# Score banks counted as free before a change of tiling in a build-time search, and the V weights on another queue

## The chip, the cores and the metric

The kernel runs on one core of one Trainium2 chip. The metric is the device time of one execution in microseconds; less is better. The core's engines are TensorE (matrix products; PE in the profile, with its weight loads as PEld), ScalarE (ACT), VectorE (DVE), GpSimd (POOL) and SyncE (SP, which here only issues DMAs). Each engine works through its own queue in order, and the engines wait for one another through semaphores.

## The reference

```python
x = A_x                                        # 1 x 2048 x 512, bf16
g = sigmoid((x * gate_w).sum(-1, keepdims=True))
q, k, v = (x @ wqkv) split into 32 heads of 16
a = softmax(q @ k.T / sqrt(16)) @ v, heads joined, @ wo
b = ((x @ w_gate) * (x @ w_up)) @ w_down       # inner width 1376
return g * a + (1 - g) * b
```

It is attention with 32 small heads over 2048 tokens beside a gated MLP, mixed by a gate per token. The matrix of probabilities has 32 x 2048 x 2048 entries, and every one of them needs an exponential: that is the bulk of the work of ScalarE and VectorE.

## The kernel before

**Units.** The scores are worked out in units of 128 keys by 512 queries for one head. One unit fills one PSUM bank (`ps` has eight; seven, `NPOOL`, are shared by everything, and the eighth, `OB`, collects the output of PV). A group `m` (32 of them, `NG`) is four heads `j` by 512 queries, with 16 blocks of keys `kt`, so there are 2048 units.

**Bursts.** Since a head has only 16 channels, TensorE runs up to four units side by side in row tiles of 32x128 (the matmul at L907, in `burst`). The mode is called "row". Everything else, the projections and the MLP (`run_fill`, matmul at L427) and PV (`pv_pack`, L1100), runs in four column tiles of 128x32, the mode "col". A spare lane of a burst can take a quarter of a product with `wo` (L433).

**Exponentials.** A unit's scores leave PSUM in one of two ways. ScalarE does `Exp` on one bank or on two neighbouring banks in one instruction (`act_step`, L968). VectorE writes a cheap approximation by integer arithmetic (`dve_exp`, L1002), which GpSimd completes with two more shifted copies (`pool_step`, L1051); PV then sums three terms in place of one. 20 or 24 units in 64 go to VectorE (`more`). As soon as the exponential has read the bank, another burst or fill may have it: `give` puts it back into `pool_free`.

**Fills.** The projections of Q, K and V, the MLP and the output products are tiles of 4 to 15 steps (`tiles`, a queue with due dates). Such a tile also holds a bank from its first step until VectorE or ScalarE has read it; at most `FILL_LIM` of them at once.

**The order.** None of this is decided on the chip. While the program is built, `_Clock` plays the engines against each other with fixed durations: a step of TensorE takes `MM` = 216 ns and `SWITCH` = 108 ns more when it changes its tiling, a result is seen `SEM` = 55 ns after its end, an exponential of n banks takes 51 + 427n ns on ScalarE and 600 ns on VectorE. Whenever an engine is free, its step function (`pe_step`, `act_step`, `dve_step`, `pool_step`) lists what it may do next, in an order of preference that constants set, and `choose` takes the entry that the next digit of `ORDER` names (0 is the first). `ORDER` was found by a search at the writer's desk. What comes out is a fixed list of instructions for each engine, with the semaphores that the data need:

```python
def ready(self, o):
    return o is not None and o.t1 + self.SEM <= self.now + 1e-6
```

An engine of the chip doesn't follow the planned times, only the planned order, and it waits on semaphores where the data are late. A burst carries a wait for each bank, on the instruction that read it last.

**The head.** The input x comes in four blocks (`x0t`, on SP's and ScalarE's queues), is transposed on TensorE with the identity `idn` and copied to `xT`; then the first Q (`wq0`) and K weights (`wk0`), then V's (`wv`), then the later x by transposing DMAs (L354 issues all loads):

```python
load("sp", "wq0", wq[:, :, 0:128], wcol(0, 128), lat=4200)
load("act", "wk0", wk[:, :, 0:128], wcol(D, D + 128), lat=4200)
load("act", "wv", wv, wcol(2 * D, 3 * D), lat=5000, prio=7)
```

`lat` is what the plan supposes for the landing. `wa` in the profile is the buffer that holds the K and V weights first and the MLP's inner values later: rows `ps<-xT,wa` are K's projection (or, with the same names, the gate's), `ps<-wa,xT` are V's.

Of the kernel before, what the change touches and what calls it, by code (L numbers as in the profile page):

```python
# [127 lines left out]
class _Clock:  # L128
# [17 lines left out]
    def ready(self, o):  # L146
        return o is not None and o.t1 + self.SEM <= self.now + 1e-6
# [56 lines left out]
def bass_gated_mix__mha_block__glu_gated_bilinear__prompt_kernel(  # L204
# [15 lines left out]
    "1100110010000010110000000000000000000000000000000100000000000000000000400000020000000010002001000000"  # L220
    "0020001000000200000001010003000000010010010000000010000001000000001001000000040000000010030000000200"
    "0000010000000000002000000000010000100000400000000001000000000000000100000000200100000000000000005000"
    "0000030200010000000001000000000001000000000001005000000020000000004000100110002000000000300000010003"
    "0000300003000000003000000100002000002000000200000040000010000000000000000100030000000000020100000001"
    "0000020000120024000000200000000400000000100000000000000000001000000000000001101000000000100000000000"
    "1000000000000000000001000001000000000400000000002000020000001000000000001000000001000100000000000100"
    "5000000000010010110000100000000000100000000000000100000000000001000000000000000000000001000000000101"
    "1100000000000020000000001000000000000000100000000000200000000000000000000100000000000000500000000000"
    "0000000002000020000010100000000000000000100000001010000000000000000000000010100000001000000400100100"
    "0400022000000000000000000000000001000000000010000000100000020000000000001100000000001000000000010000"  # L230
    "0000100100000000020010001000000002000000000002200000000000000000000010201000000000000000000000010000"
    "0000000000000000111000000030001000010040010002000010000200000000000010000000000200000000000001000000"
    "3000000100000000000001100310100000001001000000001000001001000010000001005000000000000000000000101100"
    "1220000053030000000000040000001000002000000100500000000010100000001000001000000000000001000010000000"
    "0000010000000000010000010010000000000000000000000000000000000000000000100000000100000000000001000000"
    "0100000000004000000000000400002000000001000002010000000001010001010000001001001011100000002000000420"
    "0000011010000000000001000000000000000000000000000000000000000000000000000000010000100400010001000100"
    "0000010000000102040000001000002030000000000000320012000100000011000110000500000000000110000000000100"
    "0000200000000000000000000001000000011000010000000000000000010041000000000000100000000000001100001000"
    "0000040000000000001000000000000000001000000230010000100000000001001000010000000000000000000000000111"  # L240
    "0001020000000010000000000000040000001000000000031000300000000000100000001000010000000000000000000000"
    "0100000000000001110000000000000100000000000000000010000000000100000000100100000000002200000400000002"
    "0001000000000100010100010100000200000000021000000000200000000000000000002000010000010000002004000000"
    "0000050010200000000000000020000100100003000000011110010010000003000000000000100010000000000000000000"
    "0000000000000000010000020000200000010001000000000000000000000000010000000000010000000000010000000100"
    "0000010100000000000000000000000000000001000010000001000000000000000000001005000000000000200000001040"
    "0000000000000001002000001000000000000000000040000000000001010000000000000010000000000000000000010000"
    "1000000000000000000001000000000000000010000000001000100000000400000000000000000100000300000500000000"
    "0010001000000000100020000000000002001000000000000010000002001010010000000000000000001000000000101010"
    "1303000053000200000000020000000003000100000101000110100100000001001001000110000000000000000000000"  # L250
# [12 lines left out]
MM, SWITCH, SECOND, MML = 216.0, 108.0, 10.0, 390.0  # L263
# [26 lines left out]
def _build(nc, A_x, A_wqkv, A_wo, W_gate, W_up, W_down, gate_w, out):  # L290
# [8 lines left out]
    with ExitStack() as stack:  # L299
# [59 lines left out]
        load("sp", "wq0", wq[:, :, 0:128], wcol(0, 128), lat=4200)  # L359
        load("act", "wk0", wk[:, :, 0:128], wcol(D, D + 128), lat=4200)  # L360
        load("act", "wv", wv, wcol(2 * D, 3 * D), lat=5000, prio=7)
        t_x = {}
        for ch in range(1, NCH):
            if ch == NCH - 1:
                load("sp", "wk1", wk[:, :, 128:D], wcol(D + 128, 2 * D), lat=6000)
                load("sp", "wq1", wq[:, :, 128:D], wcol(128, D), lat=6500)
                load("sp", "gw", gw[:, :], gate_w.rearrange("(kt p) -> p kt", p=128), lat=6000, allow_slow_non_contiguous=True)
            for kt in range(KD):
                load("sp", f"x{ch}{kt}", xT[:, kt, ch * 512 : (ch + 1) * 512],
                     x2[ch * 512 : (ch + 1) * 512, kt * 128 : (kt + 1) * 128], lat=3900, transpose=True)  # L370
                K.tasks["sp"][-1][4] = 1650.0
# [43 lines left out]
        const("pool", "qz0", lambda g: g.memset(QE[:, :, 1:NB, :].rearrange("p e b n -> p e (b n)").bitcast(F32), 0.0), ["wdz"], 1650, 1700)  # L415
# [23 lines left out]
        pool_free = list(range(NPOOL))  # L439
        fill_n = [0]  # L440
# [382 lines left out]
        def plan_burst(bias):  # L823
# [4 lines left out]
            banks = [b_ for b_ in pool_free]  # L828
# [106 lines left out]


# [6 lines left out]
        def act_step():  # L943
            if K.pick("act", 1):
                return True
            n = min(len(act_ready), len(pt_free) - 2 * y_out[0])
            if n < 0:
                n = 0
            if not n:
                return K.pick("act")  # L950
            us = [act_ready[0]]
            if n > 1:
                near = [x for x in act_ready if abs(x[1] - us[0][1]) == 1]
                if near and choose("a", ["2", "1"]) == "2":
# [9 lines left out]
            def done(o):  # L964
                for (u, bank, _), q in zip(us, cells):
                    give(bank, [o])

            o = K.issue("act", lambda a: a.activation(PT[:, cs, :], ps[:, bs, :], ACT.Exp, scale=math.log(2.0) / 1024.0),  # L968
                        deps, 51.0 + 427.0 * n, 176.0 + 427.0 * n, done)
# [25 lines left out]
        def dve_exp():  # L995
            if not can_dve():
# [6 lines left out]
                        [dep] + pt_rel[y], 600.0, 690.0, lambda o: (give(bank, [o]), pool_add.append((u, y, o))))  # L1003
# [66 lines left out]
        def pv_ready(it):  # L1070
            if not K.ready(it.dep):
                return False
# [4 lines left out]
        def pv_pick():  # L1077
            m = pvm[0]
            if m >= NG or m not in n_dve or not pv_open[0] or not all(K.ready(o) for o in pv_rel[0]):
                return []  # L1080
            r = []
            for j in range(4):
                for it in pvq.get((m, j), ()):
                    if pv_ready(it):
# [144 lines left out]
        def fill_tile():  # L1229

            for i, tl in enumerate(list(tiles)[: FILL_LOOK + 2 * (stat["units"] >= 4 * T * NG)]):
                d = tl.deps()
                ok = d is not None and all(K.ready(o) for o in d)
                if tl.bank is None:
# [5 lines left out]
                    if fill_n[0] < lim and len(pool_free) >= FILL_MIN:  # L1240
                        return tl
# [7 lines left out]
        def fill_begin(tl):  # L1249
            got = sorted(pool_free)  # L1250
# [154 lines left out]
        ACT_CAP, DVE_CAP, BIAS, THR_A, THR_D, LATE, EARLY, FILL_LOOK = 6, 2, 400.0, 800.0, 0.0, 12, 40, 3  # L1405
        FILL_MIN, KMIN, PT_MIN, PV_MIN, FILL_LIM, FF, FF_PT = 1, 3, 9, 4, 2, 1, 8
# [183 lines left out]
```

## Time and profile before

| | us |
|---|---|
| median of three runs | 655.16 |
| lowest, highest | 654.68, 655.42 |
| the profiled execution | 657.29 |
| its span in the profile | 655.7 |
| ScalarE's exponentials, from the first start to the last | 12.7 to 639.3 |

The span is what the profile covers, from the first instruction to the last; the execution's own time has about 1.6 us more. All times inside the profile are in microseconds from the start of the span. A row of the timeline gives the start, the time that it took (of several merged instructions, from the first start to the last end), engine, line, operation, output and inputs, and in brackets the idle time of the engine before it and who ended that. Matmuls overlap, so their own durations (0.38 us) are longer than their distance.

### The profile page before, as it was taken

The page shows a single profiled execution, that of the slowest core. Times are in us where ns is not written, and L with a number is a line of the kernel's source. Part 1 is how long each engine was busy: PE and PEld are TensorE (multiplying, and loading weights), DVE is VectorE, ACT ScalarE, POOL GpSimd, SP SyncE. Part 2 cuts the span into 40 slices and gives each one's busy share as a digit, 9 for nine tenths or more (in the row PEclk, how much of TensorE's full clock was granted, in tenths as well). Part 3 has the DMA queues.
Part 4 walks back from the last instruction along what each step waited for, and adds up shares of the span by engine and source line. Part 5 has one row for each costly group of instructions (what it writes and reads, how often), then busy time and mean ns, then how long its engine had stood idle before and what let it go on. Part 6 is the DMA issues. An engine that isn't in the chain of part 4 may idle for free.

```text
span 655.7 us, 21110 instructions
## 1 busy us (share of the span) xinstructions
PE 647.3 (99%) x8690; PEld 187.3 (29%) x8690; DVE 593.0 (90%) x1000; ACT 629.3 (96%) x772; POOL 542.7 (83%) x1397
## 2 busy tenths in 40 slices
PE   7999999999999999999999999999999999999997
PEld 3332222222222222222222232222222322222233
DVE  5999999999998898989998989999998899999994
ACT  3899999999999999999999999999999999999992
POOL 2479998888988898988788989989897898899890
PEclk8999999999999999999999999999999999999999
DMA  8930201000010100101000010100101010000101
GB/s 153 282 91 6 71 9 35 13 11 27 2 35 2 42 20 17 29 3 35 2 19 30 13 41 10 29 10 7 31 6 40 19 36 2 7 24 2 28 18 36
DMA packets 28659, 21.16 MB, mean 32 GB/s; under 512 B 16488, under 2 KB 24396, under 8 KB 28560
## 3 DMA queue, kind: packets, MB, share of 16 engines
q1 hardware_dynamic: 27216, 18.87, 10.8%
q8 instruction: 68, 1.11, 0.7%
q10 hardware_dynamic: 1344, 0.92, 0.5%
q14 instruction: 31, 0.25, 0.1%
HBM read 11.63 MB, written 2.37 MB: 21 GB/s over the span
## 4 chain that ended last, share of the span: by engine, by line
PE 60%; ACT 37%; DVE 1%; DMA 1%; issue 0%; SPq 0%; DVEq 0%
ACT PT L968 37%; PE ps L1100 21%; PE ps L427 20%; PE ps L907 17%; PE ps L433 3%; DVE PT L1002 1%; DMA wq<-in_A_wqkv_dram 1%; DMA gsm<-gscr 0%; PE ps L1211 0%; DVE gsm L592 0%; SPq L354 0%; DVE oc L1197 0%; ACT QE L710 0%; DVE usb L583 0%; DVE rec L1188 0%
## 5 line engine op out<-in xcount | busy, mean ns | idle before, releaser
L968 ACT ACTIVATE PT<-ps 128x1024 bf16<-128x1024 f32 (+1 forms) x761 | 622.9, 1050 | 5.0 <-PE ps L907 4.6
L1051 POOL INT64_ADD PT<-PT x1386 | 539.8, 409 | 96.0 <-DVE PT L1002 82.6
L1002 DVE TENSOR_SCALAR PT<-ps 128x512 int16<-128x512 f32 x708 | 461.5, 684 | 39.3 <-PE ps L907 26.7
L907 PE MATMUL ps<-QE,KK 32*128 32x512 bf16 x2048 | 253.5, 384 | 0.1
L1100 PE MATMUL ps<-PT,V 128*32 128x512 bf16 (+1 forms) x2048 | 227.9, 384 | 0.0
L1100 PE MATMUL ps<-PT,VS 128*32 128x512 f16 x1416 | 181.2, 384 | 0.0
L907 PEld LDWEIGHTS ps<-QE,KK 32*128 32x128 bf16 x2048 | 65.2, 91 | 236.9 <-ACT PT L968 184.2
L1100 PEld LDWEIGHTS ps<-PT,V 128*32 128x32 bf16 x2048 | 55.0, 95 | 63.0 <-issue 51.4
L1100 PEld LDWEIGHTS ps<-PT,VS 128*32 128x32 bf16 x1416 | 43.6, 95 | 40.6 <-issue 28.6
L427 PE MATMUL ps<-wd,wa 128*32 128x512 bf16 x704 | 54.5, 382 | 0.0
L427 PE MATMUL ps<-xT,wu 128*32 128x512 bf16 x704 | 53.4, 383 | 0.1
L427 PE MATMUL ps<-xT,wg 128*32 128x512 bf16 x704 | 53.3, 383 | 0.0
L622 DVE TENSOR_TENSOR usb<-ps,omg 128x512 bf16<-128x512 f32 x44 | 30.0, 683 | 2.0 <-PE ps L427 1.9
L649 DVE TENSOR_TENSOR wa<-ps,usb 128x512 bf16<-128x512 f32 x44 | 30.1, 683 | 1.4 <-PE ps L427 1.2
L433 PE MATMUL ps<-wo,OT 32*128 32x512 bf16 x80 | 30.8, 384 | 0.2
L427 PE MATMUL ps<-xT,wq 128*32 128x512 bf16 x256 | 20.3, 396 | 2.1 <-DMA wq<-in_A_wqkv_dram 2.1
L427 PE MATMUL ps<-xT,wa 128*32 128x512 bf16 x272 | 21.4, 398 | 0.1
L1197 DVE COPY oc<-ps 128x512 f32<-128x512 f32 x31 | 21.1, 682 | 0.3
L427 PEld LDWEIGHTS ps<-wd,wa 128*32 128x32 bf16 x704 | 15.5, 95 | 19.4 <-issue 11.8
L427 PEld LDWEIGHTS ps<-xT,wg 128*32 128x32 bf16 x704 | 13.8, 95 | 18.7 <-issue 11.3
L427 PEld LDWEIGHTS ps<-xT,wu 128*32 128x32 bf16 x704 | 13.1, 95 | 18.6 <-issue 12.7
L427 PE MATMUL ps<-wa,xT 128*32 128x512 bf16 x256 | 17.8, 384 | 0.0
(73 smaller groups left out, 142.8 us busy)
## 6 DMA issues: line engine op xcount, KB each, us to landing
rb<-rscr SPq DMA_DIRECT2D x16, 256.0 KB
QE<-Qr SPq DMA_DIRECT2D x120, 16.0 KB, 1.8
oc<-oc SPq DMA_DIRECT2D x60, 32.0 KB, 1.9
out_dram<-ost SPq DMA_DIRECT2D x12, 128.0 KB, 1.7
wu<-in_B_w_up_dram SPq DMA_DIRECT2D x1, 1376.0 KB, 7.5
wg<-in_B_w_gate_dram SPq DMA_DIRECT2D x1, 1376.0 KB, 9.6
wd<-in_B_w_down_dram SPq DMA_DIRECT2D x1, 1280.0 KB, 14.0
wa<-in_A_wqkv_dram ACTq DMA_DIRECT2D x1, 512.0 KB, 7.0
```

The costliest lines, as they stand in the source:

```text
L427: r = pe.matmul(ps[32 * i : 32 * i + 32, bank, :], w, x_, start=s0, stop=s1, tile_position=(0, 32 * i), skip_group_check=True)
L433: return pe.matmul(ps[:, bank, :], lhs[32 * q : 32 * q + 32, :], rhs[32 * q : 32 * q + 32, :], start=s0, stop=s1, tile_position=(32 * q, 0 ...
L622: return v.tensor_tensor(usb[:, st["s"], :], ps[:, bank, :], omg[:, cf, :], ALU.mult)
L649: return v.tensor_tensor(hT[:, f, :], ps[:, bank, :], usb[:, u_at[cf, f][0], :], ALU.mult)
L907: return lambda pe: pe.matmul(ps[:, bank, :], KK[32 * j : 32 * j + 32, b, kt * 128 : (kt + 1) * 128], QE[32 * j : 32 * j + 32, p, b, :], s ...
L968: o = K.issue("act", lambda a: a.activation(PT[:, cs, :], ps[:, bs, :], ACT.Exp, scale=math.log(2.0) / 1024.0), deps, 51.0 + 427.0 * n, 17 ...
L1002: o = K.issue("dve", lambda v: v.tensor_scalar(PT[:, y, :].bitcast(I16), ps[:, bank, :], BIAS16, 0.0, ALU.add, ALU.max), [dep] + pt_rel[y] ...
L1051: return g.int64_add(PT[:, zl, :].bitcast(I64), PT[:, sl, :].bitcast(I64), w)
L1100: return lambda pe: pe.matmul(ps[32 * it.j : 32 * it.j + 32, OB, :], lhs, it.rhs, start=s0, stop=s1, tile_position=(0, 32 * it.j), skip_gr ...
L1197: K.task("dve", deps, lambda v: v.tensor_copy(oc[:, p, :], ps[:, OB, :]), 600.0, 690.0, done, 0)
```

## The change

It has two parts. **The plan.** An exponential now gives its banks back `AHEAD` = 90 ns before its result would be seen (`soon`), with the true time kept as `bank_hard`. `avail` lists such a bank at once where TensorE would change its tiling to use it, and only from the true time on where it wouldn't. PV in a change from "row" may look 90 ns ahead in the same way (`pv_ready`, `pv_pick`). Three constants of the preferences differ (`BIAS` 600 for 400, `EARLY` 80 for 40, `FILL_LIM` 3 for 2), and `ORDER` is another string, from a search with 768 variants (its 31 lines of digits are left out of the diff below). The waits on the chip are still made from the data, so no bank is touched before it has been read.

**The head.** `wv` is issued by SP behind `wq0`, ahead of the transposing loads, in place of by ScalarE behind `wk0`. Suppositions on landings differ (`lat`). GpSimd's fill of `QE` with zeros (`qz0`) waits for VectorE's `idn`.

```diff
-    def ready(self, o):
-        return o is not None and o.t1 + self.SEM <= self.now + 1e-6
+    def ready(self, o, ahead=0.0):
+        return o is not None and o.t1 - ahead + self.SEM <= self.now + 1e-6
...
-MM, SWITCH, SECOND, MML = 216.0, 108.0, 10.0, 390.0
+MM, SWITCH, SECOND, MML, AHEAD = 216.0, 108.0, 10.0, 390.0, 90.0
...
-        load("sp", "wq0", wq[:, :, 0:128], wcol(0, 128), lat=4200)
-        load("act", "wk0", wk[:, :, 0:128], wcol(D, D + 128), lat=4200)
-        load("act", "wv", wv, wcol(2 * D, 3 * D), lat=5000, prio=7)
+        load("sp", "wq0", wq[:, :, 0:128], wcol(0, 128), lat=3800)
+        load("act", "wk0", wk[:, :, 0:128], wcol(D, D + 128), lat=3800)
+        load("sp", "wv", wv, wcol(2 * D, 3 * D), lat=5200)
...
-                     x2[ch * 512 : (ch + 1) * 512, kt * 128 : (kt + 1) * 128], lat=3900, transpose=True)
+                     x2[ch * 512 : (ch + 1) * 512, kt * 128 : (kt + 1) * 128], lat=(6000, 5000, 4200, 3900)[kt] if ch == 1 else 3900, transpose=True)
...
-        const("pool", "qz0", lambda g: g.memset(QE[:, :, 1:NB, :].rearrange("p e b n -> p e (b n)").bitcast(F32), 0.0), ["wdz"], 1650, 1700)
+        const("pool", "qz0", lambda g: g.memset(QE[:, :, 1:NB, :].rearrange("p e b n -> p e (b n)").bitcast(F32), 0.0), ["wdz", "idn"], 1650, 1700)
...
-        def give(bank, ops):
+        def give(bank, ops, hard=-1e9):
             bank_rel[bank] = ops
+            bank_hard[bank] = hard
             pool_free.append(bank)
@@ plan_burst
-            banks = [b_ for b_ in pool_free]
+            banks = avail("row")
@@ burst
-            got = sorted(pool_free)
+            got = sorted(avail("row"))
...
+        def avail(md):
+
+            soft = mode[0] is not None and (mode[0] == "row") != (md == "row")
+            return [b_ for b_ in pool_free if soft or bank_hard[b_] <= K.now + 1e-6]
+
+        def soon(o, banks):
+            def fn():
+                for b_ in banks:
+                    give(b_, [o], o.t1 + K.SEM)
+            K.at(o.t1 + K.SEM - AHEAD, fn)
@@ act_step
-                        deps, 51.0 + 427.0 * n, 176.0 + 427.0 * n, done)
+                        deps, 51.0 + 427.0 * n, 176.0 + 427.0 * n)
+            soon(o, banks)
@@ dve_exp
-                        [dep] + pt_rel[y], 600.0, 690.0, lambda o: (give(bank, [o]), pool_add.append((u, y, o))))
+                        [dep] + pt_rel[y], 600.0, 690.0, lambda o: pool_add.append((u, y, o)))
+            soon(o, [bank])
@@ pv_pick
-            if m >= NG or m not in n_dve or not pv_open[0] or not all(K.ready(o) for o in pv_rel[0]):
+            ahead = AHEAD if mode[0] == "row" else 0.0
+            if m >= NG or m not in n_dve or not pv_open[0] or not all(K.ready(o, ahead) for o in pv_rel[0]):
@@ fill_tile
-                    if fill_n[0] < lim and len(pool_free) >= FILL_MIN:
+                    if fill_n[0] < lim and len(avail("col")) >= FILL_MIN:
@@ fill_begin
-            got = sorted(pool_free)
+            got = sorted(avail("col"))
...
-        ACT_CAP, DVE_CAP, BIAS, THR_A, THR_D, LATE, EARLY, FILL_LOOK = 6, 2, 400.0, 800.0, 0.0, 12, 40, 3
-        FILL_MIN, KMIN, PT_MIN, PV_MIN, FILL_LIM, FF, FF_PT = 1, 3, 9, 4, 2, 1, 8
+        ACT_CAP, DVE_CAP, BIAS, THR_A, THR_D, LATE, EARLY, FILL_LOOK = 6, 2, 600.0, 800.0, 0.0, 12, 80, 3
+        FILL_MIN, KMIN, PT_MIN, PV_MIN, FILL_LIM, FF, FF_PT = 1, 3, 9, 4, 3, 1, 8
```

More of the change, by code (lines that the diff above doesn't have):

```diff
@@ L225 @@
[L225 to L229, printed above, removed]
@@ new lines @@
+    "2000000000002000000002000000000001000001040001000050000000100000100000002000100000010000002001100000"
+    "3000001000000000000200000040000000000000000001010100000200002000000000000010000000000010050000500000"
+    "1000000010100000000000000000000000000000000000001000000100000000100500000000011200000000100500000000"
+    "0000000000000010000000010200000000000000010000001000000000100000000000100000000100000050000000000000"
+    "0102000000000000000000000010000010000000100000001000000000100001000000000100004000201100000005010000"
@@ new lines @@
+    "0000000121000000000000000001000000100000000001000000200100000000000000000000000000001000000000100000"
+    "0000000000100100001001020000000003001300000000000000100000000000000010001100000000000000000000000010"
+    "0100010050010400000000000000101000000000000000000000000000000101101001000000000001000100001000000000"
+    "0010100000010000000001000000010004010000000000000001000001000000000120010100001000000001000000100000"
+    "0100000000100000000102000000100000004000000000000001102000100001000000100000000000000010000000100000"
@@ new lines @@
+    "0001000001000000000000000000000000000000000001010010000000100000100000000001000012000000004000000100"
+    "0000000001000000000000000000000000000001000000000000000000000000000000000000010000100100000000001000"
+    "0100100000000000000000030000100000100000100000000000000000000000010400010000000003042001000000002000"
+    "0030000000010000000000000200000000000100030010000100000000001300000000000000000001000000000001100000"
+    "0020000200000000000010200100100000010010200000000000030000000200000010000000010000010000000000000101"
@@ new lines @@
+    "0000000100000000100000000000010110000100000000001000000010000000000200000000010000000100040000001100"
+    "0000000110002210000000000000000000010000000100000000100000001100002005000000010000000010000001000000"
+    "0000000100000000000100000011000000000000000000003100000210001020000000400000000001030000005000000000"
+    "0000000000020010000001000000000020000100000000100001020000050000000000000000000000000000001001000010"
+    "0000101000000010110000002110001000000500000000000000000000030000100000100000000010400000000010000000"
@@ new lines @@
+    "1000000001010000001030000200000000000200000000000000000000000000010000000000000000000000003000101005"
+    "0000000000005000000000000100101000000000000000010000000000100000000000000000000000110000000010000102"
+    "0000001000000000110000110000000010000000010000000004002001000000001000000000000010000000100040000011"
+    "0010000001001000000001000001000000000100000200000100000000121000000000000010000000100010000010000200"
+    "0100000000000001000000000000000000001000000000000000000000000000010200000000220010040000000000003500"
@@ L251 @@
+    "0000000300000000010200000000001000000010000000010000000000000102001000001000000010050000000000000000"
+    "0001000001000000000000000000000000000000000000000000000000000000000000000"
 )
@@ L439, in _build @@
         pool_free = list(range(NPOOL))
+        bank_hard = {b_: -1e9 for b_ in range(8)}
         fill_n = [0]
@@ L1067, in _build, with pv_ready @@
         hold = [0.0]
-        def pv_ready(it):
-            if not K.ready(it.dep):
+        def pv_ready(it, ahead):
+            if not K.ready(it.dep, ahead):
                 return False
@@ L1083, in pv_pick @@
                 for it in pvq.get((m, j), ()):
-                    if pv_ready(it):
+                    if pv_ready(it, ahead):
                         r.append(it)
```

33 lines of the change are left out of this document (4 added, 29 removed).

## The prediction

> **What bounds the kernel now.** First the page: the span and the busy shares, then the chain that ended last.
>
> ```profile
> span 655.7 us, 21110 instructions
> PE 647.3 (99%) x8690; PEld 187.3 (29%) x8690; DVE 593.0 (90%) x1000; ACT 629.3 (96%) x772; POOL 542.7 (83%) x1397
> ...
> PE 60%; ACT 37%; DVE 1%; DMA 1%; issue 0%; SPq 0%; DVEq 0%
> ```
>
> TensorE and ScalarE are both nearly full, and the chain changes between them: neither is a bound alone. The page says that a busy PE need not be PE at its peak, so the next view is the timeline of TensorE in the middle of the run, with the start of each group of up to four matmuls in the first column.
>
> ```profile
> 88.09 0.39 PE L907 MATMUL ps<-QE,KK 32*128 32x512 bf16 x3
> 88.41 0.39 PE L1100 MATMUL ps<-PT,V 128*32 128x512 bf16 x1
> 88.41 0.40 PE L1100 MATMUL ps<-PT,VS 128*32 128x512 f16 x3
> 88.64 0.39 PE L1100 MATMUL ps<-PT,V 128*32 128x512 bf16 x3
> 88.64 0.38 PE L1100 MATMUL ps<-PT,VS 128*32 128x512 f16 x1
> 89.00 0.39 PE L907 MATMUL ps<-QE,KK 32*128 32x512 bf16 x4
> ...
> 302.18 0.38 PE L1100 MATMUL ps<-PT,VS 128*32 128x512 f16 x1
> ...
> 302.50 0.39 PE L907 MATMUL ps<-QE,KK 32*128 32x512 bf16 x3
> ```
>
> L907 is a burst of scores (row tiles of 32x128), L1100 a pack of PV (column tiles of 128x32). Column to column takes 0.23 us (88.41 to 88.64), either change of tiling 0.32 (88.09 to 88.41; 302.18 to 302.50). A change thus costs about 0.10 us, and a burst between two packs 0.32 + 0.32 - 0.22 = 0.42 us, however many scores it holds. At 89.00 the change took 0.36. Why, the rows of ScalarE and of the weight loads at that place say:
>
> ```profile
> 86.85 2.10 ACT L968 ACTIVATE PT<-ps 128x1024 bf16<-128x1024 f32 x2
> ...
> 89.00 0.10 PEld L907 LDWEIGHTS ps<-QE,KK 32*128 32x128 bf16 x4 [0.47 <-ACT PT L968]
> ```
>
> The exponential ended at 86.85 + 2.10 = 88.95, and the weights followed 0.05 us later: that is what a released bank needs to reach TensorE. Here the bank was late by about 0.04 us. The waits (us in total, times, longest) show that this is not the usual case:
>
> ```profile
> PEld ps L907 <- ACT PT L968: 184.2, 435, 0.5
> ...
> PEld ps L907 <- issue: 27.8, 67, 0.4
> ...
> PEld ps L907 <- DVE PT L1002: 15.9, 39, 0.5
> ...
> PEld ps L433 <- PE ps L907: 22.2, 54, 0.4
> ...
> PEld ps L433 <- issue: 9.8, 23, 0.4
> ```
>
> The mean before L907 is 184.2/435 = 0.42 us where ScalarE is named and 27.8/67 = 0.41 where nobody is. A true wait for a bank would make the first longer. So TensorE mostly waits for its own change, with the bank already free: it is the busy one, and what it does is set by the order worked out at build time. The rows also count bursts: 435 + 67 + 39 + 54 + 23 = 618 (L433 rides ahead of the scores in a burst), and a few smaller rows left out, so at most 2048/618 = 3.3 scores a burst where four lanes exist.
>
> ScalarE's room comes from its own groups, kept apart by shape:
>
> ```profile
> L968 ACT ACTIVATE PT<-ps 128x1024 bf16<-128x1024 f32 x579 | 553.0, 1155 | 5.0 <-PE ps L907 4.6
> ...
> L968 ACT ACTIVATE PT<-ps 128x512 bf16<-128x512 f32 x182 | 110.3, 717 | 0.0
> ```
>
> It idles 5.0 us in 579 + 182 = 761 instructions. These durations overlap (their sum, 663.3, is more than the span), so the true room may be larger, but this is what the trace shows. When the exponentials begin and end, and VectorE's share, say the line's own view and the page's row:
>
> ```profile
> L968 ACT ACTIVATE PT<-ps x761: 591/1132/1318, 12.7 to 639.3; 128x1024 bf16<-128x1024 f32 x148, 128x512 bf16<-128x512 f32 x43
> ```
> ```profile
> L1002 DVE TENSOR_SCALAR PT<-ps 128x512 int16<-128x512 f32 x708 | 461.5, 684 | 39.3 <-PE ps L907 26.7
> ```
>
> Last, the head, where DMA is the bound: timeline, DMA table and windows (length, busy PE, PEld, DVE, ACT, POOL, then the granted clock, DMA share, GB/s).
>
> ```profile
> 1.67 0.44 SPq L354 DMA_DIRECT2D wq<-in_A_wqkv_dram  x1
> ...
> 2.01 1.38 POOL L415 MEMSET QE<- 128x1536 f32 x1
> ...
> 2.16 11.23 SPq L354 DMA_TRANSPOSE xT<-in_A_x_dram  x8
> 2.19 0.47 ACTq L354 DMA_DIRECT2D wa<-in_A_wqkv_dram  x1
> ...
> 2.49 0.98 DVE L398 TENSOR_SCALAR idn<-rb 128x128 bf16<-128x128 f32 x1
> ...
> 4.52 0.45 PEld L463 LDWEIGHTS ps<-idn,PT 128*128 128x128 bf16 x8 [0.21 <-DMA PT<-in_A_x_dram]
> ...
> 4.59 1.18 ACT L473 ACTIVATE xT<-ps 128x512 bf16<-128x512 bf16 x2 [0.97 <-PE ps L463]
> ...
> 7.64 1.76 PE L427 MATMUL ps<-xT,wq 128*32 128x512 bf16 x16 [2.07 <-DMA wq<-in_A_wqkv_dram]
> ...
> 10.86 1.46 PE L427 MATMUL ps<-wa,xT 128*32 128x512 bf16 x20
> ...
> 16.27 1.04 PE L427 MATMUL ps<-xT,wa 128*32 128x512 bf16 x16
> ```
> ```profile
> wa<-in_A_wqkv_dram ACTq DMA_DIRECT2D x1, 512.0 KB, 7.0
> ...
> wq<-in_A_wqkv_dram SPq DMA_DIRECT2D x1, 384.0 KB, 4.3
> ...
> xT<-in_A_x_dram SPq DMA_TRANSPOSE x12, 3.8
> ...
> wq<-in_A_wqkv_dram SPq DMA_DIRECT2D x1, 128.0 KB, 5.8
> ```
> ```profile
> 4.00:5.60 1.60, 1.57 (x16) 0.86 (x13) 1.30 (x10) 1.01 (x2) 0.19 (x1) 1.00 0.93 240
> 5.60:7.60 2.00, 0.00 (x0) 0.00 (x0) 0.00 (x0) 0.17 (x1) 0.00 (x0) 1.00 1.26 173
> 7.60:9.50 1.90, 1.86 (x20) 0.94 (x24) 0.06 (x1) 0.00 (x0) 0.00 (x0) 0.56 1.34 203
> 9.50:11.27 1.77, 1.77 (x21) 0.79 (x17) 0.69 (x1) 0.12 (x1) 0.00 (x0) 0.51 0.89 186
> ```
>
> TensorE stood still for 2.07 us up to 7.64 for the first Q weights, 128 KB that took 5.8 us while the 512 KB of V weights ran beside them from ScalarE's queue; the later Q weights, three times as large, took 4.3. And after that gap the granted clock was about half for 3.67 us.
>
> **The change, part by part.**
>
> *V weights behind wq0 on SP.* One issue of about 0.47 us leaves ScalarE's queue and enters SP's. ScalarE's next work is at 4.59, so it gains nothing. On SP it passes all twelve transposes, the rest of K and Q, and the large weights; each is issued about 0.5 us later. wq0 loses its rival. Its landing is bounded by 5.8 us (no gain) and 2.9 us (half of that); I take the 4.3 us of the larger, later transfer, the nearest row. Issued at 1.67, it lands at 6.0. The other input, the transposed x, is ready when ScalarE ends at 4.59 + 1.18 = 5.8, so that is the next thing late and the gain cannot pass 1.8. **-1.6 us** (bounds 0 and -1.8).
>
> *The clock.* The half clock followed the gap. With a gap of some 0.4 us in place of 2.07 I expect it not to be taken back: 1.90 x 0.44 + 1.77 x 0.49 = 1.70 us, **-1.7** (bounds 0 and -1.7). The Trainium skill ("TensorE: Matmul & The Clock Gate", Part 1: The HAM clock gate) says otherwise in detail: half rate comes after at least one idle window of about 3.4 us, and the window runs free of the kernel's start. The trace differs in that 2.07 us were enough; by the free window, keeping the clock would be luck of the phase, and this term would be 0.
>
> *V's own landing.* With both terms the first V matmuls, at 10.86 now, come at 10.86 - 3.3 = 7.5. V weights issued at 2.16 land between 2.16 + 4.3 = 6.5 and 2.16 + 7.0 = 9.2. Midway is 7.8: **+0.3** (bounds 0 and 1.7). The fourth transpose of the second chunk is issued near 2.16 + 0.5 + 3 x 1.4 = 6.9 (11.23/8 = 1.4 each), lands at the median of 3.8 by 10.7, and is wanted at 16.27 - 3.3 = 13.0: nothing; behind V's bytes on the same queue it could take 1.2 more than that slack.
>
> *idn before the fill of QE.* VectorE's idn took 0.98 us while GpSimd's fill of 1.38 ran. Now the fill waits for it. The last transposes wait for x at 4.52 in any case, and GpSimd's first real work comes after the first scores: 0. GpSimd is in order: only the small add0 stands behind the fill.
>
> *The search and its bank rule.* Nothing is added to the chip: the same matmuls, exponentials and adds, in another order with other banks. What can fall is the number of bursts, at 0.42 us each. A bank may be planned 0.09 us earlier across a change, and the change takes 0.10; the 0.05 of the release are in the plan before and after. So a bank may come some 0.01 us later than planned; where it comes later still, the burst waits at the head of TensorE's queue, with the PV packs and projections behind it, and ScalarE and VectorE behind those. From how many releases could a burst profit? 761 exponentials and 708 of VectorE in 627 us (12.7 to 639.3) are 2.3 a microsecond, so 0.21 fall into 0.09 us: 618 x 0.21 = 130 bursts might take one score more, 130/3.3 = 39 fewer bursts, 16 us of TensorE. That is the upper end. ScalarE cannot follow so far: its idle time is 5.0 us, and fuller bursts that it can't take up only lie in banks. (VectorE, 90% busy, could take some of its share, but each unit there adds two quarters of a PV pack; I hold the split of 1340 to 708.) The lower end is 0, or a loss (below). I take ScalarE's 5.0: **-5.0 us**. The other constants (BIAS 600, EARLY 80, three fill banks) change only what the search may choose; a third fill bank takes a score bank away, so some of the gain may be spent there.
>
> Sum: -1.6 - 1.7 + 0.3 - 5.0 = -8.0 us. The profiled execution took 657.29 us (span 655.7 and 1.6 around it), 2.1 more than the median of 655.16. It should come to 649.3, and the median to **647.2 us**.
>
> **The rivals.** (1) The clock isn't kept: the head gives 1.6 alone, V is then early enough: -6.6, 648.6 us. For it speaks that the trace holds one gap alone and doesn't show how short a gap is let pass; against it that the clock was full in 4.00:5.60 and fell only after the gap.
> (2) ScalarE and TensorE are both as full as seven banks allow, and the search only moves waits about: the steady part gives nothing, the head 3.0: 652.2 us, and 653.6 with the clock lost too. For it speaks 99% and 96%.
> (3) Slower: the banks come late. The plan's margin shrinks to about 0.01 us. If half of 618 bursts meet a bank as late as that at 89.00, 0.04 us each, 309 x 0.04 = 12.4 us are lost and none of it comes back, because the queue is in order: 659.6 us. It decides from 8.0/618 = 0.013 us mean lateness upward. For it speaks that exponentials take 591 to 1318 ns, which no plan foresees; against it the mean wait of 0.42, which shows almost no lateness in a plan made by the same reckoning.
> (4) More than forecast: ScalarE's overlapped durations hide room, and the upper end of the bursts holds: -3.0 - 16 = -19.0, 636.2 us.
> (5) The move doesn't do what it is for: wq0 still lands at 5.8 us, because x and the K weights, not V's, hold it up. The head gives nothing, the rest its 5.0: 650.2 us.
>
> **How the numbers follow.** Forecast 0.38, (1) 0.18, (2) 0.17, (3) 0.18, (4) 0.05, (5) 0.04. About 0.2% or 1.3 us is what a measurement here can tell from no change. The forecast, (1), (4), (5) and two thirds of (2) are faster by more: 0.76; the rest of (2) is the same: 0.06; (3) is slower: 0.18. The range from 641 to 658 leaves out (4) and some two thirds of (3), 0.17, and holds the bounds of head and clock.
>
> **What would show it.** In the changed profile: the idle time before the first Q matmul under 0.6 us and its start near 6.0; a clock of 1.00 from there; V's matmuls near 7.8; fewer waits counted at L907 and L433 together (near 605); ScalarE's idle time before L968 under 5 us; and the mean wait before L907 still 0.42. A mean of 0.45 or more would mean rival (3). The same number of bursts would mean (2). The prediction is wrong if the head is shorter and the rest, from the first scores to the last, is not.

## The result, and the profile after

The change makes the kernel faster by two tenths of a per cent, and not by the 1.2% that was forecast.

| | before | after |
|---|---|---|
| median, 20 executions of each | 655.23 | 654.07 us |
| lowest, highest | 654.52, 656.08 | 652.97, 654.82 |
| the profiled execution | 657.29 | 653.78 |
| its span | 655.7 | 651.8 |

The ratio is 0.998 (95%: 0.9973 to 0.9987), 1.2 us. First the page of the changed kernel: span, busy shares, chain.

```profile
span 651.8 us, 21202 instructions
...
PE 644.6 (99%) x8706; PEld 188.1 (29%) x8706; DVE 598.2 (92%) x1008; ACT 627.7 (96%) x790; POOL 549.4 (84%) x1421
...
PE 85%; ACT 10%; DVE 4%; DMA 0%; issue 0%
```

ScalarE's share of the chain fell from 37% to 10%, as if TensorE alone were now the bound. The runs below show that this reading is wrong. Next the head, in TensorE's timeline of after, and V's weights in its DMA table (KB, and us from issue to landing).

```profile
6.37 1.18 PE L427 MATMUL ps<-xT,wq 128*32 128x512 bf16 x16
7.38 1.03 PE L427 MATMUL ps<-xT,wa 128*32 128x512 bf16 x16
8.25 1.25 PE L427 MATMUL ps<-wa,xT 128*32 128x512 bf16 x20
9.43 0.40 PE L909 MATMUL ps<-QE,KK 32*128 32x512 bf16 x4
```
```profile
wa<-in_A_wqkv_dram SPq DMA_DIRECT2D x1, 512.0 KB, 5.3
```

The first Q product came at 6.37 instead of 7.64, with no wait for its weights, and V's at 8.25 instead of 10.86, straight behind K's product and with no wait either. The same row of before for the first scores, and the stretch from first to last burst, by the view of the tile QE (durations in ns, then the starts of the first and the last score):

```profile
12.25 0.40 PE L907 MATMUL ps<-QE,KK 32*128 32x512 bf16 x4
```
```profile
L907 PE MATMUL ps<-QE,KK x2048: 371/384/385, 12.2 to 638.2; 32*128 32x512 bf16 x187
```
```profile
L909 PE MATMUL ps<-QE,KK x2048: 371/384/386, 9.4 to 633.8; 32*128 32x512 bf16 x187
```

So the profiled executions differ by -2.8 us before the first scores, by about -1.6 us between the first and the last burst (626.0 to 624.4), and by +0.5 us behind it (17.5 to 18.0): together the 3.9 us of the spans. The prediction had -3.0, -5.0 and nothing for the tail. Now the exponentials by shape (count, then busy time and mean ns, then the engine's idle time ahead of them) and the waits ahead of a burst:

```profile
L977 ACT ACTIVATE PT<-ps 128x1024 bf16<-128x1024 f32 x553 | 531.2, 1157 | 2.4 <-PE ps L909 2.1
L977 ACT ACTIVATE PT<-ps 128x512 bf16<-128x512 f32 x226 | 135.5, 706 | 2.9 <-PE ps L909 2.8
L1012 DVE TENSOR_SCALAR PT<-ps 128x512 int16<-128x512 f32 x716 | 466.3, 684 | 35.5 <-PE ps L909 20.9
```
```profile
PEld ps L909 <- ACT PT L977: 207.2, 483, 0.5
PEld ps L909 <- DVE PT L1012: 16.0, 37, 0.7
PEld ps L909 <- issue: 11.7, 29, 0.4
PEld ps L433 <- PE ps L909: 19.5, 48, 0.4
PEld ps L433 <- issue: 8.5, 20, 0.4
```

ScalarE's idle time did not fall (5.0 to 2.4 + 2.9 = 5.3 us), and the mean wait behind ScalarE rose only from 0.42 to 207.2/483 = 0.43. The sum of the counts, 617 where 618 were, doesn't count bursts well: a burst whose scores come apart waits twice. By the lists of instructions that the plans give, the order has 646 bursts before and 627 after.

### The profile page after: what moved, and what is told of

Its sections match the earlier page's. It is cut to its first block, busy times and chain, and to the rows that moved or that the text cites. A ratio compares the mean times of both kernels' runs of the same rounds, so it can differ in the third digit from the quotient of the medians.

```text
span 651.8 us, 21202 instructions
## 1 busy us (share of the span) xinstructions
PE 644.6 (99%) x8706; PEld 188.1 (29%) x8706; DVE 598.2 (92%) x1008; ACT 627.7 (96%) x790; POOL 549.4 (84%) x1421
## 3 DMA queue, kind: packets, MB, share of 16 engines
HBM read 11.63 MB, written 2.37 MB: 21 GB/s over the span
## 4 chain that ended last, share of the span: by engine, by line
PE 85%; ACT 10%; DVE 4%; DMA 0%; issue 0%
PE ps L1112 31%; PE ps L427 25%; PE ps L909 25%; ACT PT L977 10%; PE ps L433 3%; DVE PT L1012 2%; DVE V L555 1%; DMA PT<-in_A_x_dram 0%; DVE VS L563 0%; DVE OT L1191 0%; PE ps L465 0%; DVE KK L489 0%; PE ps L1223 0%; PE ps L389 0%; DVE Qr L534 0%
## 5 line engine op out<-in xcount | busy, mean ns | idle before, releaser
L1062 POOL INT64_ADD PT<-PT x1410 | 546.5, 407 | 84.4 <-DVE PT L1012 72.7
L1012 DVE TENSOR_SCALAR PT<-ps 128x512 int16<-128x512 f32 x716 | 466.3, 684 | 35.5 <-PE ps L909 20.9
L909 PE MATMUL ps<-QE,KK 32*128 32x512 bf16 x2048 | 248.1, 384 | 0.4 <-DVE PT L1012 0.2
L1112 PE MATMUL ps<-PT,VS 128*32 128x512 f16 x1432 | 187.2, 384 | 0.0
L909 PEld LDWEIGHTS ps<-QE,KK 32*128 32x128 bf16 x2048 | 64.1, 91 | 238.1 <-ACT PT L977 207.2
L427 PE MATMUL ps<-wd,wa 128*32 128x512 bf16 x704 | 52.2, 382 | 0.9 <-DVE PT L1012 0.9
L433 PE MATMUL ps<-wo,OT 32*128 32x512 bf16 x68 | 26.2, 385 | 0.1
L427 PEld LDWEIGHTS ps<-xT,wg 128*32 128x32 bf16 x704 | 13.8, 95 | 19.2 <-issue 10.9
```

Of the source, the lines that this page charges most:

```text
L427: r = pe.matmul(ps[32 * i : 32 * i + 32, bank, :], w, x_, start=s0, stop=s1, tile_position=(0, 32 * i), skip_group_check=True)
L433: return pe.matmul(ps[:, bank, :], lhs[32 * q : 32 * q + 32, :], rhs[32 * q : 32 * q + 32, :], start=s0, stop=s1, tile_position=(32 * q, 0 ...
L909: return lambda pe: pe.matmul(ps[:, bank, :], KK[32 * j : 32 * j + 32, b, kt * 128 : (kt + 1) * 128], QE[32 * j : 32 * j + 32, p, b, :], s ...
L1012: o = K.issue("dve", lambda v: v.tensor_scalar(PT[:, y, :].bitcast(I16), ps[:, bank, :], BIAS16, 0.0, ALU.add, ALU.max), [dep] + pt_rel[y] ...
L1062: return g.int64_add(PT[:, zl, :].bitcast(I64), PT[:, sl, :].bitcast(I64), w)
L1112: return lambda pe: pe.matmul(ps[32 * it.j : 32 * it.j + 32, OB, :], lhs, it.rhs, start=s0, stop=s1, tile_position=(0, 32 * it.j), skip_gr ...
```

## The experiments

**The two parts apart.** Four kernels, timed against the same executions of before: before once more, before's order with the new head, the new order with the old head, and after.

```diff
 e2_head: before, with the list of instructions changed after the planning
+P.ops.remove(ld["wv"]); ld["wv"].eng = "sp"
+P.ops.insert(P.ops.index(ld["wq0"]) + 1, ld["wv"])
+c["qz0"].deps.append(c["idn"])          # qz0 moved behind idn in the list
 e3_order: after, with the same two taken back
+ld["wv"].eng = "act"                    # behind ScalarE's first operation
+c["qz0"].deps.remove(c["idn"])
```

> The kernel before once more, for a second profile and the spans and clocks of many executions of it. The profiled execution of before took 657.29 us, 2.1 more than its median. Theory A (the half clock of 3.4 us in its head is an accident of that execution): the new profile and most runs show a granted clock nearer 1.000 and spans near 653.6. Theory B (the half clock belongs to this head): mean clock 0.997 in nearly all runs. The time is the same as before: ratio 1.000.

> The kernel before with its own order, every instruction of the five engines as planned, but with V's weights issued by SP behind wq0 and the fill of QE behind idn, as in the change. Theory A (the head of most executions of before keeps its clock): first burst near 9.5 us in the profile, the median falls by the wait for wq0 alone, 0.5 to 1.5 us (654.0 +- 0.5). Theory B (the head always lost 2.8 us as in the profile): the median falls by 2.5 to 3 us (652.5). If ScalarE were not the bound behind the head, the gain would vanish on the way: 655.2.

> The changed kernel with its own new order, but V's weights issued by ScalarE behind wk0 and the fill of QE not waiting, as before. Theory A (the new order is worth only what ScalarE's work falls by: 553 exponentials of two banks and 226 of one against 579 and 182): 0 to -1.6 us, so 653.6 to 655.2. Rival (the new order gives the 5 us that the plan counts, and the head costs the rest): 650. Rival (the tight banks cost more than the order wins): 656.

> The changed kernel once more beside the two halves. 654.1 us, ratio 0.998. If the halves add up, the ratios of head alone and order alone multiply to this one within 0.001.

Against 655.07 us for 35 executions of before: e1 654.89, ratio 0.9997 (0.9989 to 1.0006); e2 654.37, 0.9991 (0.9982 to 1.0); e3 655.63, 1.0012 (1.0003 to 1.002); e4 654.31, 0.9991 (0.9982 to 1.0). The new head alone thus gives 0.7 us, all that the whole change gives here, with 1.0 at the edge of both intervals. The new order alone gives nothing: with the old head it was 0.6 us slower, outside the 653.6 to 655.2 that was expected. The halves don't add up either: their ratios multiply to 0.9991 x 1.0012 = 1.0003, and e4 has 0.9991, apart by more than the 0.001 that was set, though not by more than the intervals allow. The tile view of e2 and e3:

```profile
L907 PE MATMUL ps<-QE,KK x2048: 371/384/385, 9.6 to 635.6; 32*128 32x512 bf16 x187
```
```profile
L909 PE MATMUL ps<-QE,KK x2048: 371/384/385, 12.4 to 636.8; 32*128 32x512 bf16 x187
```

The stretch follows the order (626.0 in e2, 624.4 in e3), the first scores follow the head. Why does the head give 2.8 us in a profile and 0.7 in a median? Both profiled executions of before (657.29 and e1's 657.27) had the half clock and lie 2.1 and 2.4 us above their medians. The granted clock, listed as a mean for each execution, is 0.997 or less in 4 of 74 executions of before, all of them at 656.58 us or more, and in 3 of e3's 12; the rest have 0.998 to 1.0. With V's weights on SP (after, e2, e4, e11) none of 54 was below 0.998. The half clock is real and costs about 2 us, but it is rare, and the prediction put its whole price into the median. Nor is a profiled execution a fair draw: of the four with before's loads (before, e1, e3, e12) three had the half clock, of the other 95 with the same loads (in e1, e3, e12 and beside the runs) five.

The tail is the order's too. The groups of PV from the last burst on, before and then after (count, busy us, mean ns):

```profile
L1100 PE MATMUL ps<-PT,VS 128*32 128x512 f16 x13 | 1.6, 383 | 0.0
L1100 PE MATMUL ps<-PT,V 128*32 128x512 bf16 (+1 forms) x11 | 1.5, 379 | 0.0
```
```profile
L1112 PE MATMUL ps<-PT,V 128*32 128x512 bf16 (+1 forms) x24 | 2.6, 383 | 0.0
L1112 PE MATMUL ps<-PT,VS 128*32 128x512 f16 x16 | 1.9, 380 | 0.0
```

Four of the 40 in after began at 633.51, ahead of the last burst and still running. So the new order leaves 36 of these matmuls for the end in place of 24: three packs more at 0.22 us, 0.7 us. From last burst to end were 17.5, 17.4 and 17.2 us in before's order (before, e1, e2) and 18.0, 18.0 and 18.3 in the new one (after, e3, e4).

**What sets the pace between the bursts.** Either ScalarE is the bound of that stretch, or TensorE is, with its late banks. So work was taken from one engine and then from the other, the order untouched.

```diff
 e5_after_496, e6_before_496 (e7: 480): ScalarE works on W of 512 queries
-a.activation(PT[:, cs, :], ps[:, bs, :], ACT.Exp, ...)
+a.activation(PT[:, cs, 0:W], ps[:, bs, 0:W], ACT.Exp, ...)
 e8_after_dve480: VectorE on 480 of 512
-v.tensor_scalar(PT[:, y, :].bitcast(I16), ps[:, bank, :], ...)
+v.tensor_scalar(PT[:, y, 0:480].bitcast(I16), ps[:, bank, 0:480], ...)
 all: one fill on GpSimd at the start zeroes the columns left out
```

These kernels leave out part of the exponentials, so their output is not the whole product; only the time is read.

> The changed kernel, same order, but ScalarE's exponentials cover 496 of the 512 queries of a unit (the other 16 columns keep older values, set to zero at the start). In the trace of the changed kernel ScalarE's exponentials end 917 ns apart for two banks and 490 for one where they follow each other, though they start 904 and 477 apart; the plan counts 905 and 478. 16 columns less take about 27 and 13 ns off, so that ScalarE keeps the plan's pace with a little room. Theory A (ScalarE's true pace is what the order's gain was lost to): first to last burst falls from 624.5 us to 616 +- 2, in all near 646. Rival B (the tight banks or the changes of tiling cost TensorE the time): it stays at 623 or more, in all 653. Rival C (VectorE is late): likewise.

> The kernel before with the same cut. Theory A: first to last burst falls from 625.9 us by less than in the changed kernel, to 621 +- 1.5, since its plan counts 5.7 us more; in all near 650. The difference between the two kernels grows from 1.2 us to 4 or more. Rivals B and C: 625 or more, and the difference stays near 1.

> The changed kernel with 480 of 512 queries on ScalarE: twice the cut. Theory A: with 496 ScalarE is already fast enough for the plan, so little more is won: first to last burst 0 to 2.5 us below that with 496. If it falls in proportion again (by 7 us or more), ScalarE alone sets the pace and no other limit is near.

> The changed kernel with VectorE's exponentials on 480 of 512 queries and ScalarE's whole: 33 ns off each of 716. Theory A: first to last burst falls by less than 1.5 us (from 624.5), because ScalarE has the same work at the same pace. Rival C (VectorE's banks are the late ones): it falls by 4 us or more.

e5 took 647.27 us, 0.9879 (0.9859 to 0.9899) of before; e6 648.14, 0.9897 (0.9878 to 0.9917); e7 647.73 and e8 653.6, the last two from one execution each. Tile view of e5 and e6, and e5's chain:

```profile
L909 PE MATMUL ps<-QE,KK x2048: 374/384/386, 9.8 to 627.2; 32*128 32x512 bf16 x187
...
PE 92%; DVE 5%; DMA 1%; issue 0%; ACT 0%; SPq 0%; DVEq 0%
```
```profile
L907 PE MATMUL ps<-QE,KK x2048: 374/384/385, 9.8 to 629.5; 32*128 32x512 bf16 x187
```

Three per cent off ScalarE shorten the stretch by 7.0 us in the new order and by 6.3 in the old. As much again gives nothing more (618.3 us in e7), so there the bound is TensorE. Six per cent off VectorE give 0.4 us. ScalarE is the bound of both kernels here, and TensorE's own bound lies 6 to 7 us below it. But the distance between the orders grew only from 1.6 to 2.3 us, where 4 or more was expected of it.

Why ScalarE, when its rows seemed to leave room? The windows of before say it (length, busy PE, PEld, DVE, ACT, POOL, then clock, DMA share, GB/s):

```profile
140.00:240.00 100.00, 99.97 (x1353) 28.14 (x1352) 91.59 (x149) 100.00 (x124) 85.21 (x221) 1.00 0.08 21
240.00:340.00 100.00, 99.93 (x1335) 28.03 (x1331) 91.24 (x150) 100.00 (x129) 84.92 (x222) 1.00 0.06 17
340.00:440.00 100.00, 99.93 (x1362) 28.27 (x1358) 90.76 (x148) 100.00 (x125) 87.71 (x225) 1.00 0.08 23
```

For 300 us ScalarE is busy all the time; in 40 to 635 us its idle time comes to 1.0 us in all. Four of the 5.0 us on its group lie outside that, nearly all ahead of it, where the first scores come slowly. And its pace is slower than its starts suggest. Two rows of ScalarE's timeline of after, each of two merged pairs, with the same unbroken chain of pairs between them:

```profile
69.66 2.08 ACT L977 ACTIVATE PT<-ps 128x1024 bf16<-128x1024 f32 x2
```
```profile
75.09 2.16 ACT L977 ACTIVATE PT<-ps 128x1024 bf16<-128x1024 f32 x2
```

From the first instruction of one row to the first of the other are six steps, and so from last to last: the starts are (75.09 - 69.66)/6 = 0.905 us apart, the ends (77.25 - 71.74)/6 = 0.918. The plan counts 0.905 (51 + 2 x 427 ns). Over all queued instructions of before the ends are 0.917 us apart for a pair (some 560 of them, nine in ten within 0.915 to 0.919) and 0.490 for a single bank, where the plan has 0.478. So ScalarE's work is 579 x 0.917 + 182 x 0.490 = 620.1 us before, and 553 x 0.917 + 226 x 0.490 = 617.8 after: 2.3 us less, because eight units more went to VectorE (716 for 708), and that is about what the stretch could gain. The stretch gained 1.6; ScalarE's idle time in 40 to 635 us rose from 1.0 to 1.6, which makes up the difference. Most of the 1.6 lies in this window of after, where before has 100.00:

```profile
340.00:440.00 100.00, 98.97 (x1358) 28.77 (x1350) 93.22 (x149) 98.88 (x128) 88.51 (x230) 1.00 0.08 23
```

Each pair split into two singles costs 2 x 0.490 - 0.917 = 0.063 us, and the new order has 44 singles more; so eight units fewer, 8 x 0.459 = 3.7 us, less 22 x 0.063 = 1.4, are the 2.3. The Trainium skill ("Perfetto Trace Analysis", Optimizing Scalar/DVE Operations) gives about 51 ns for what each ScalarE instruction on PSUM costs beside its elements, and advises larger operations where the engine is full; the trace agrees in kind, with 63.

**Both relieved.** If TensorE's order holds what the plan says of it, the two orders should come apart when neither ScalarE nor VectorE bounds them.

```diff
 e9_after_both, e10_before_both: ScalarE on 496 of 512 queries, VectorE on 480
```

> The changed kernel with 496 of 512 queries on ScalarE and 480 on VectorE, so that neither holds a bank longer than the plan counts. With ScalarE's cut alone, first to last burst took 617.4 us (plan 616.5), and the chain then ran over VectorE in places. Theory A (nothing but the paces of the two evacuating engines keeps TensorE from the new order's plan): 613 to 614.5 us, that is the plan less the 3 ns by which a change of tiling is faster than planned. Rival B (the tight banks cost TensorE time by themselves): 616.5 or more.

> The kernel before with the same two cuts (619.6 us from first to last burst with ScalarE's alone, plan 622.3). Theory A: 618.5 to 619.5, so that the two orders stand 5 to 6 us apart, as in their plans, once neither ScalarE nor VectorE is late. Rival B: the distance stays at 2 to 3.

Here 16 columns of the probabilities are zero in every unit, and the kernel's own test of the softmax sums sends it through its slow general path afterwards (24.7 ms). Only the part of the trace that follows the plan is read:

```profile
L909 PE MATMUL ps<-QE,KK x2048: 374/384/386, 9.8 to 625.8; 32*128 32x512 bf16 x187
```
```profile
L907 PE MATMUL ps<-QE,KK x2048: 374/384/385, 10.9 to 630.0; 32*128 32x512 bf16 x187
```

616.0 and 619.1 us, 3.1 apart, where the plans have 616.5 and 622.3. A change of tiling takes 0.321 us between starts (back to "col" 0.322) and not the 0.324 (216 + 108 ns) of the plan. Over some 1250 changes that is 3 us, and the old order is 3 us better on the chip than its plan. The new one should have gained as much, hence the 613 to 614.5 that was expected; it only comes to its plan. So 3 us of the planned 5.8 are there for TensorE alone, and of these 1.6 are left with ScalarE at full work.

Most of the rest is in the trace of e9, at two places. At 380.44 a product of the MLP starts 1.49 us behind the step before it, where 0.23 is usual, because its bank was still VectorE's; at 370.14 the second part of a burst starts 0.85 us behind the first, for the same reason. Together they cost about 1.9 us, by estimate from these distances; before's order has 0.3 us of this kind in e10 and nothing longer. After has the first of the two as well, at 384.83, shortly ahead of ScalarE's idle times in the window above (386.04 and 387.35). The waits show it so (us in total, times, longest):

```profile
PE ps L427 <- DVE PT L1012: 0.9, 1, 0.9
```

Ahead of it VectorE was late by one instruction: the product `OT<-oc,rb` at 382.18 took 2.00 us in after, with a median of 0.74. In all seven traces of the new order the longest of these 15 products takes 2.00 to 2.31 us, in the seven of before's order at most 0.98. Why it takes so long there, no run shows.

Late banks are for the most part a consequence of the same pace. Counted over all changes from "col" to "row", from the first matmul of one group to the first of the next, those that came more than 5 ns behind the usual 0.321 us are 80 in before (2.8 us together) and 134 in after (5.4 us). With ScalarE at 496 columns, and the same 90 ns rule, only 19 (0.5 us) are left.

**Which edit of the head.** Each on before's order:

```diff
 e11_before_wv: only V's weights to SP, behind wq0
+P.ops.remove(ld["wv"]); ld["wv"].eng = "sp"
+P.ops.insert(P.ops.index(ld["wq0"]) + 1, ld["wv"])
 e12_before_qz: only the fill of QE behind idn
+c["qz0"].deps.append(c["idn"])          # qz0 moved behind idn in the list
```

> The kernel before with only V's weights moved to SP behind wq0 (the fill of QE not waiting). Both together gave -0.7 us. Theory H1 (the queue): 654.4, wq0 in time (idle under 0.5 us before the first Q matmul), clock 1.000. Theory H2 (the fill of QE, not the queue, held up the head): 655.1 and the wait for wq0 still there in the profile.

> The kernel before with only the fill of QE waiting for idn, V's weights on ScalarE's queue. H1: as before, 655.1, the first Q matmul near 7.6 us in the profile. H2: 654.4 and the first Q matmul near 6.3.

e11 took 654.57 us, 0.9988 (0.9978 to 0.9998) of 655.32; e12 655.43, 0.9998 (0.999 to 1.0007). The gain of the head is all from V's weights, as far as intervals of 0.6 us either way tell. TensorE's timeline of e11, then e12's with its windows:

```profile
6.36 1.05 PE L427 MATMUL ps<-xT,wq 128*32 128x512 bf16 x16
...
9.28 0.39 PE L907 MATMUL ps<-QE,KK 32*128 32x512 bf16 x4
```
```profile
8.00 1.05 PE L427 MATMUL ps<-xT,wq 128*32 128x512 bf16 x16 [1.59 <-DMA wq<-in_A_wqkv_dram]
...
5.60:7.60 2.00, 0.81 (x2) 0.00 (x0) 0.00 (x0) 0.59 (x1) 0.00 (x0) 1.00 1.27 205
7.60:9.50 1.90, 1.50 (x28) 0.87 (x32) 0.41 (x1) 0.00 (x0) 0.00 (x0) 1.00 1.20 185
```

In e12 the Q weights came later than in before (8.00), behind a gap of 1.59 us, and the clock stayed at 1.00. Its earlier matmuls ran until 6.41 where before's ended at 5.57. So a late weight costs its own wait, and the clock only now and then on top. How late the weights are in a usual execution no profile shows: the first scores came at 10.9 in e12, 1.6 us behind e11's, and the medians are 0.9 us apart. In e10, with V's weights on ScalarE's queue and one fill more on GpSimd, the first Q product came at 6.17, and it was V's weights that were waited for:

```profile
9.74 1.26 PE L427 MATMUL ps<-wa,xT 128*32 128x512 bf16 x20 [1.40 <-DMA wa<-in_A_wqkv_dram]
```

## Why the prediction was wrong

**The direction was right, the size was not.** 647.2 us was forecast, with -8.0 us; the time is 654.07, inside the range, with -1.2.

*V weights, -1.6: held in the profile, mis-sized in the median.* The Q weights landed early, no wait was left, and e11 shows that this edit alone makes the head. The first Q product came at 6.37; 6.0 was forecast. The prediction took the landing of before's one profile as usual, and the median gain of 0.7 us says that it isn't. Why V's place matters, that its bytes hold up the Q weights, is argued: before, e1, e3 and e12 had the first Q product at 7.64 to 8.00, but e6 and e10, with V on the same queue, had it at 6.29 and 6.17. Those two have a fill on GpSimd ahead of the rest, and no run tells its effect from chance.

*The clock, -1.7: shown in the profile, mis-sized in the median.* The clock stayed at 1.00. But the term was taken from an execution that was not typical. The prediction saw that it lay 2.1 us above the median and carried the whole gain over all the same. This is the first step that failed: head together -2.8 in the profile, -0.7 in the median.

*V's own landing, +0.3:* V's products came at 8.25 where 7.8 was forecast, but not by their weights: no wait stands ahead of them, and TensorE came from K's product. The term was 0, and that the times lie near each other is luck. *idn ahead of the fill, 0:* e12 gave +0.1 us, within its interval.

*The search, -5.0: the step that failed most.* "I take ScalarE's 5.0" read idle time as room. That idle time is not in the steady part: 1.0 us of it lies between 40 and 635 us. What the stretch could gain was ScalarE's work, and the prediction held that fixed: "I hold the split of 1340 to 708". The new order has 1332 to 716, which is where the 2.3 us come from, and by that also 16 PV matmuls more, against "nothing is added to the chip". The stretch gained 1.6, the tail gave 0.5 to 1.1 back, and by the medians the order as a whole is worth nothing (e4 beside e2) to 0.5 us (the result's 1.2 less e2's 0.7), and less than nothing with the old head (e3). The count of bursts did fall, by 19 of the 39 that were the upper end, and at 0.42 us each that is 8.0 us of TensorE; the plan keeps 5.8 of it, the chip 3.1 when ScalarE is out of the way, and 1.6 when it isn't. By the prediction's own signs too, ScalarE's idle time (5.3 us, not under 5) and the waits (617, not near 605) spoke against this term. What the 90 ns rule, the constants and the search each have in this, no run separates.

*The rivals.* (2), the steady part giving nothing, is the nearest by mechanism, "both as full as seven banks allow"; e5 and e6 show that it is ScalarE's pace, not the banks. (3), late banks, is there in small: 134 late changes, 5.4 us, where before has 80 and 2.8, at a mean wait of 0.43, under the 0.45 that was set for it. (1), the clock not kept, did not happen in after. (4) was out of reach: ScalarE had no hidden room. (5), that the move does nothing, is refuted by e11, though narrowly: its interval is 0.9978 to 0.9998.

Open is why the new order with the old head (e3) was 0.6 us slower than before, though its stretch is 1.6 shorter and its tail 0.6 longer. Three of its twelve executions had the lower clock, which may be a part of it; what the rest is, no run separates.

No kernel that does the whole work was faster than the changed one by more than the intervals. What the experiments point to is an order searched with ScalarE's true pace, 0.917 and 0.490 us, and with fewer single banks; it wasn't tried.

## What to carry to other kernels

Before an engine's idle time is counted as room, look at where in the run it lies: four of five us of idle at the ends are no room in the middle, and an engine with 96% of the span can be at 100% of the stage that matters. The chain of waits can name one engine while another sets the pace; taking a few per cent of work from each, with the order kept, tells them apart in one run each. And a term read from a profile that lies above the median belongs into the median only as often as it occurs; here the profiled executions had it far more often than the others.

## What the runs showed of the hardware

ScalarE's back-to-back exponentials start 0.905 us apart and end 0.917 apart, so that durations in a full queue grow, up to 1.318 us for a pair, and the engine's pace is read from the ends. After a gap of 2.07 (before), 2.37 (e1) and 2.31 us (e3) TensorE's clock was halved, after one of 1.59 us (e12) and one of 1.40 (e10) it was not. By the record of the clock in the traces the half clock lasted 3.41 us each time (7.83 to 11.24 in before). The 3.41 us just ahead of it held the whole gap, and TensorE was busy for 1.1 to 1.3 us of them. In e12, where the record sets in at 6.98, a stretch of the same length from there has 2.4 us of work and the one ahead 2.7: the gap lay across both. In e10 the gap lay in one stretch, with 2.0 us of work. The Trainium skill ("TensorE: Matmul & The Clock Gate", Part 1: The HAM clock gate) asks for at least one idle window of about 3.4 us, running free of the kernel; the gaps measured here are shorter than that and still halved the clock, while their changing effect fits a window that runs free. The 128 KB of the first Q weights took 5.8 to 6.2 us from issue to landing in before, e1, e3 and e12, with V's weights on ScalarE's queue, and 4.5 and 4.0 in e6 and e10 with them on the same queue; with V's behind them on SP they took 4.0 (after) to 5.1 us (e5, e9).
